# Keeping the convolution's buffers alive across stages, with Q computed row block by row block

## The chip, the cores and the metric

The kernel runs on one core of a Trainium2 chip. The metric is the device time of one execution in microseconds (us); the figure for a kernel is the median of several executions. TensorE (PE) does the matmuls, with its weight loads listed separately (PEld); VectorE (DVE) and ScalarE (ACT) take results out of PSUM and do the elementwise work; SyncE's queue (SP) issues every transfer. The transfers themselves run on 16 DMA engines.

## The reference

One branchformer layer over two sequences, B = 2, T = 4000, D = 512, convolution width K = 31, all in bfloat16. Cut to what matters:

```python
xa = layernorm(x)
q, k, v = split(xa @ w_qkv, 3)
p = softmax(q @ k.T * D**-0.5)
glob = (p @ v) @ w_att_out
h = gelu(layernorm(x) @ w_mlp_in)
u, g = h[..., :D], layernorm(h[..., D:])
gc = depthwise_conv(g, dw_csgu)          # 31 taps along t, each channel by itself
loc = (u * gc) @ w_mlp_out
m = concat(glob, loc)                    # 1024 channels
m = m + depthwise_conv(m, dw_merge)
out = x + m @ w_merge
```

There are two depthwise convolutions: the gate convolution over 512 channels of `g`, and the merge convolution over 1024 channels of `m`.

## The kernel before

For each of the two batches the kernel goes through the same stages, with all of a stage's time steps done before the next one starts:

- P1: load x, layer normalisation in groups of 8 tiles of 128 rows (statistics on VectorE), transpose on TensorE, copy by ScalarE into `xnT` (channels on partitions). Batch 1's P1 is emitted with batch 0's final projection.
- P3: `g` by matmul with `w_in` (`pg`), Gelu, normalisation, store to DRAM (`g_d`); `u` by matmul into `uT`; the gate convolution; then the matmul with `w_mo` and the store of `loc_d`.
- P2: the Q and V projections. W_q times W_k transposed is folded into one matrix `A_sb`, and W_v times the output projection into `Wvo_sb`, so that keys are `xnT` itself.
- Attention: for each of 32 blocks of 128 rows the scores S (8 tiles of up to 512 columns, `pS`), the row maximum on VectorE, Exp on ScalarE in two halves into `Pm`, a DMA transpose of `Pm` into `PT`, and 32 accumulating matmuls of `PT` with `v_sb` (`pO`), whose result `at` is stored to `glob_d`. The emission order puts the scores of the next block, and two tiles of the one after, ahead of PV of the present block.
- P5: the merge convolution over `loc_d` and then `glob_d` into `mconvT`, and the final matmul with `w_mg` (`po`), to which x is added (`xt`, `ot`).

A convolution goes over chunks of 128 channels: 4 chunks for the gate, 8 for the merge. For a chunk, `depthwise` loads `mch` (41 overlapping windows of 128 time steps, 128 channels; 1312 KB in runs of 256 bytes) and eight `tz` tiles. A `tz` tile holds, for 16 channels, the banded matrix that turns the convolution of one channel into one matmul; it is read from a small DRAM array `zz` with overlapping rows, 512 KB a time. Each channel is then one matmul of 41 columns with a weight load of its own (L129), VectorE copies 12 channels at a time into `cm` (L136), and 41 transposes per chunk (L144) bring the result back to channels on partitions.

Every transfer is issued by SP, in program order, with its waits ahead of it. The order within an engine is what a list scheduler made of the emitted program, guided by when tiles come free. Memory is given out by pools that are opened and closed like a stack. The convolution's pools (`mch` 3 buffers, `cm` 2, `tz` 10) are opened anew in each stage and so take addresses that the stage before was using; loads into them can't start before those tenants are done. The same holds for `w_in`, which is placed where P1's buffers were. `qT`, the whole Q of a batch, takes 32 KB per partition all through attention.

Of the kernel before, what the change touches and what calls it, by code (L numbers as in the profile page):

```python
# [11 lines left out]
BF = mybir.dt.bfloat16  # L12
F32 = mybir.dt.float32
PSUM = bass.MemoryType.PSUM

P = 128
# [3 lines left out]
SEG = 128  # L20
LEAD = 112
EPS = 1e-5
CG = 16
TZB = 10
LNG = 8


# [5 lines left out]
def kernel(  # L33
# [40 lines left out]
    A_sb = const.tile([P, KC, D], BF, name="A_sb")  # L74
    Wvo_sb = const.tile([P, KC, D], BF, name="Wvo_sb")

    zz = tc.dram_tile([LEAD + CT * SEG + P], BF, name="zz")
    g_d = [tc.dram_tile([TP, D], BF, name=f"g_d{b}") for b in range(B)]
    glob_d = [tc.dram_tile([TP, D], BF, name=f"glob_d{b}") for b in range(B)]
# [23 lines left out]
    def ln_group(small, src, i0, ni, tagp):  # L103
# [7 lines left out]
        nc.vector.reciprocal(rstd[:, :ni], rstd[:, :ni])  # L111
        return mv, rstd

    def depthwise(sc, ch_base, cc, m_pool, cm_pool, tz_pool, ps_pool):
        src_tl = m_pool.tile([P, NB, P], BF, name="mch")
        nc.sync.dma_start(src_tl[:], halo_chunk_src(sc, cc))
        cm = cm_pool.tile([P, P, NBP], BF, name="cm")
        tzs = []
        for g0 in range(0, P, CG):
            tz = tz_pool.tile([P, CG * SEG], BF, name="tz")  # L120
            nc.sync.dma_start(tz[:], hankel_src(ch_base + cc * P + g0, CG))
            tzs.append(tz)
        for c0 in range(0, P, PB):
            cn = min(PB, P - c0)
            pc = ps_pool.tile([P, PB, NB], F32, name="pc")
            for c in range(c0, c0 + cn):
                tz = tzs[c // CG]
                o = (c % CG) * SEG
                nc.tensor.matmul(  # L129
                    pc[:, c - c0, :],  # L130
                    tz[:, o:o + P],
                    src_tl[:, :, c],
                    start=True,
                    stop=True,
                )
            nc.vector.tensor_copy(cm[:, c0:c0 + cn, :NB], pc[:, :cn, :])  # L136
        return cm
# [13 lines left out]
                emit(SO * n, v, pT[:, nn - 1, P - 1 - PADT:P - 1 - PADT - v:-1], 0)  # L151

    def emit_p1(b, xnT, xp, io, small, ps1):
        x_all = xp.tile([P, NT, D], BF, name="x_all")
        if rem:
            nc.vector.memset(x_all[:, nfull, :], 0.0)
            nc.sync.dma_start(x_all[:rem, nfull, :], x[b, nfull * P:T, :])
        for i0 in range(0, NT, LNG):
            ni = min(LNG, NT - i0)
            nf = min(i0 + ni, nfull) - i0  # L160
            if nf > 0:
                nc.sync.dma_start(
                    x_all[:, i0:i0 + nf, :],
                    x[b, i0 * P:(i0 + nf) * P, :].rearrange("(n p) d -> p n d", p=P),
                )
        for i0 in range(0, NT, LNG):
            ni = min(LNG, NT - i0)
            mv, rstd = ln_group(small, x_all, i0, ni, "x")
            for i in range(i0, i0 + ni):
                r = min(P, T - i * P)  # L170
                xn = io.tile([P, D], BF, name="xn")
                nc.vector.tensor_scalar(
                    xn[:r], x_all[:r, i, :], mv[:r, i - i0, 0:1],
                    rstd[:r, i - i0:i - i0 + 1], ALU.subtract, ALU.mult,
                )
                pt = ps1.tile([P, KC, P], BF, name="pt1")
                for k in range(KC):
                    nc.tensor.transpose(
                        pt[:, k, :r], xn[:r, k * P:(k + 1) * P], ident[:r, :r]
                    )  # L180
                nc.scalar.copy(xnT[:, :, i * P:i * P + r], pt[:, :, :r])  # L181
# [72 lines left out]
    def emit_p3(b, xnT):  # L254
        with tc.tile_pool(name=f"ug{b}", bufs=1) as ug_pool, tc.tile_pool(
# [7 lines left out]
            with tc.tile_pool(name="p3ga", bufs=1) as gap:  # L263
# [24 lines left out]
                for e in range(KC):  # L288
                    for t0 in range(0, T, 512):
# [13 lines left out]
            with tc.tile_pool(name="p3m", bufs=3) as mp, tc.tile_pool(  # L303
                name="p3cm", bufs=2
            ) as cmp_, tc.tile_pool(name="p3tz", bufs=TZB) as tzp, tc.tile_pool(
                name="p3pc", bufs=2, space=PSUM
            ) as psc, tc.tile_pool(name="p3pt", bufs=2, space=PSUM) as pst:
                for cc in range(KC):
                    cm = depthwise(g_d[b], 0, cc, mp, cmp_, tzp, psc)

                    def emit(t0, ln, src, nblk, cc=cc):
                        dst = uT[:, cc, t0:t0 + ln]
                        if nblk:
                            dst = dst.rearrange("p (n s) -> p n s", s=SO)
                        nc.vector.tensor_tensor(dst, src, dst, ALU.mult)

                    conv_to_dlayout(cm, pst, emit)
# [20 lines left out]
                            nc.vector.tensor_copy(l_all[:r, i, :], pl[:r, :])  # L338
                    store_rows(loc_d[b], l_all, i0, ni)

    def emit_p2(b, xnT, qT, v_sb):
        with tc.tile_pool(name="p2ps", bufs=4, space=PSUM) as ps2:
            cnt = 0
            for e in range(KC):
                for t0 in range(0, T, 512):
                    w = min(512, T - t0)
                    pq = ps2.tile([P, 512], F32, name="pq")
                    for k in range(KC):
                        nc.tensor.matmul(  # L349
                            pq[:, :w],  # L350
                            A_sb[:, k, e * P:(e + 1) * P],
                            xnT[:, k, t0:t0 + w],
                            start=(k == 0),
                            stop=(k == KC - 1),
                        )
                    if cnt % 2 == 0:
                        nc.scalar.copy(qT[:, e, t0:t0 + w], pq[:, :w])
                    else:
                        nc.vector.tensor_copy(qT[:, e, t0:t0 + w], pq[:, :w])
                    cnt += 1  # L360
            for i in range(NA):
                r = min(RC, T - i * RC)
                pv = ps2.tile([P, 512], F32, name="pq")
                for k in range(KC):
# [7 lines left out]
                if cnt % 2 == 0:  # L372
# [3 lines left out]
                cnt += 1  # L376

    def emit_attention(b, qT, kT, v_sb):
# [4 lines left out]
        with tc.tile_pool(name="p4s", bufs=2) as sp, tc.tile_pool(  # L383
# [5 lines left out]
        ) as psS, tc.tile_pool(name="p4psT", bufs=(1 if DMAT else 3), space=PSUM) as psT, tc.tile_pool(  # L389
            name="p4psO", bufs=2, space=PSUM  # L390
        ) as psO:
            state = {}
            LEADT = 2 if NS > 4 else 0

            def emit_S(i, j0, j1):
                r = min(RC, T - i * RC)
                if i not in state:
                    state[i] = dict(
                        S=sp.tile([P, T], F32, name="S_sb"),
                        mt=small.tile([P, NS], F32, name="mt"),  # L400
                    )
                S_sb, mt = state[i]["S"], state[i]["mt"]
# [68 lines left out]
            def emit_PV(i):  # L471
# [16 lines left out]
                )  # L488
                del state[i]

            emit_S(0, 0, NS)
            emit_softmax(0)
            if NA > 1:
                emit_S(1, 0, LEADT)
            for i in range(NA):
                if i + 1 < NA:
                    emit_S(i + 1, LEADT, NS)
                    emit_softmax(i + 1)
# [2 lines left out]
                emit_PV(i)  # L501

    def emit_merge_conv(b, mconvT):
        with tc.tile_pool(name="p5m", bufs=3) as mp, tc.tile_pool(
            name="p5cm", bufs=2
        ) as cmp_, tc.tile_pool(name="p5tz", bufs=TZB) as tzp, tc.tile_pool(
            name="p5pc", bufs=3, space=PSUM
        ) as psc, tc.tile_pool(name="p5pt", bufs=3, space=PSUM) as pst:
            for h in (1, 0):
                for cc in range(KC):  # L510
                    cm = depthwise((glob_d, loc_d)[h][b], D + h * D, cc, mp, cmp_, tzp, psc)
# [36 lines left out]
    for b in range(B):  # L548
        emit_p3(b, xnT)
        at_ctx = ExitStack()  # L550
        at_pool = at_ctx.enter_context(tc.tile_pool(name=f"att{b}", bufs=1, side="right"))
        qT = at_pool.tile([P, KC, T], BF, name="qT")
        v_sb = at_pool.tile([P, NA, D], BF, name="v_sb")
        emit_p2(b, xnT, qT, v_sb)
        emit_attention(b, qT, xnT, v_sb)
        at_ctx.close()
        xn_ctx.close()

# [48 lines left out]
```

## Time and profile before

| | before |
|---|---|
| time, median of 5 | 1795.91 us (1792.29 to 1796.77) |
| profiled execution | span 1789.3 us, mean granted TensorE clock 0.905 |
| PE busy | 1657.7 us (93%) |
| DVE, ACT busy | 841.5 us (47%), 574.7 us (32%) |
| transfers | 257.39 MB, mean 144 GB/s; q1 busy 55.5% of 16 engines' span |
| scores L407, PV L477 | 440.7 and 456.9 us busy |
| conv matmuls L129, transposes L144 | 245.2 and 107.1 us busy |

A row of the page's groups gives line, engine, operation, output and inputs, shape and count, then busy time and mean duration, then the time that the engine stood idle just before and what ended it. A busy PE is not PE at its peak: matmuls are pipelined, and their durations overlap, so the spacing of their starts is the price of one. The page's part 2 cuts the span into 40 slices of 44.7 us; a digit is a busy share in tenths. A line of the sums over stretches has start and end, length, the busy time of PE, PEld, DVE, ACT and POOL with the number of instructions in brackets, then the granted clock, the share of the DMA engines and GB/s. A line of the chain of waits has start, length and what the end of the program was waiting for at that time.

### The profile page before, as it was taken

The numbers are of one execution on the slowest core, as the hardware profiler recorded it, in microseconds if no ns is written. First come the engines' busy times: TensorE is split into PE (matmuls) and PEld (weight loads), VectorE is DVE, ScalarE is ACT, GpSimd is POOL, SyncE is SP. The second block draws the span as 40 slices with busy tenths as digits, with TensorE's granted clock in tenths as the row PEclk, the third lists the DMA queues.
The fourth block names the chain that finished last, engine by engine and source line by source line (L and its number), as shares of the span: only waits on it lengthen the run. The fifth ranks groups of instructions, "written<-read, shape, count | busy, mean of one in ns | idle before, by whom it ended". The sixth has DMA issues, their size and how long they took to land.

```text
span 1789.3 us, 25506 instructions
## 1 busy us (share of the span) xinstructions
PE 1657.7 (93%) x10166; PEld 918.6 (51%) x10292; DVE 841.5 (47%) x2093; ACT 574.7 (32%) x782; POOL 13.8 (1%) x72
## 2 busy tenths in 40 slices
PE   5899999999999997978978999999999999978799
PEld 3368444444444443877443774444444444457764
DVE  7636344444444442444747453544444444424333
ACT  6740333333333332212048213333333333321210
POOL 0000000000000000000000000000000000000000
PEclk9986999999999999655979889999999999985569
DMA  5695205444444447998753941244445444489964
GB/s 157 223 228 175 92 0 103 80 86 94 86 80 80 94 91 167 320 315 262 216 205 99 262 143 62 36 94 80 80 89 94 84 80 83 96 262 297 300 220 140
DMA packets 473063, 257.39 MB, mean 144 GB/s; under 512 B 394898, under 2 KB 446801, under 8 KB 472944
## 3 DMA queue, kind: packets, MB, share of 16 engines
q1 hardware_dynamic: 472944, 255.76, 55.5%
q8 instruction: 80, 1.31, 0.3%
q14 instruction: 39, 0.32, 0.1%
HBM read 156.73 MB, written 33.46 MB: 106 GB/s over the span
## 4 chain that ended last, share of the span: by engine, by line
PE 43%; DMA 5%; ACT 2%; DVE 1%; issue 1%; SPq 0%; ACTq 0%; DVEq 0%
PE pS L407 12%; PE pO L477 12%; PE po L528 6%; DMA tz<-zz 4%; PE pc L129 4%; PE pTc L144 3%; PE pq L365 2%; PE pg L328 2%; PE pq L349 2%; PE pg L293 1%; PE pg L273 1%; DVE cm L136 1%; ACT xnT L181 1%; DMA w_in<-in_w_mlp_in_dram 0%; DMA w_mg<-in_w_merge_dram 0%
## 5 line engine op out<-in xcount | busy, mean ns | idle before, releaser
L414 DVE TENSOR_SCALAR_CACHE_REDUCE S_sb<-pS,mt 128x512 f32<-128x512 f32 (+1 forms) x448 | 329.7, 736 | 291.6 <-PE pS L407 243.6
L477 PE MATMUL pO<-v_sb,PT 128*128 128x512 bf16 (+2 forms) x2008 | 456.9, 379 | 6.5 <-DMA PT<-Pm 4.4
L407 PE MATMUL pS<-xnT,qT 128*128 128x512 bf16 (+2 forms) x2008 | 440.7, 374 | 3.7 <-DVE v_sb L375 1.5
L437 ACT ACTIVATE Pm<-S_sb,nb 128x2048 bf16<-128x2048 f32 (+3 forms) x128 | 250.1, 1954 | 365.1 <-DVE nb L428 365.1
L477 PEld LDWEIGHTS <-PT 128*128 128x128 bf16 (+2 forms) x2048 | 199.4, 98 | 266.4 <-issue 28.7
L407 PEld LDWEIGHTS <-qT 128*128 128x128 bf16 (+1 forms) x2048 | 195.1, 98 | 233.5 <-issue 14.3
L136 DVE CAST cm<-pc 128x492 bf16<-128x492 f32 (+1 forms) x264 | 171.5, 657 | 254.0 <-PE pc L129 254.0
L129 PE MATMUL pc<-mch,tz 128*128 128x41 bf16 x3072 | 245.2, 250 | 47.3 <-DMA tz<-zz 46.1
L129 PEld LDWEIGHTS <-tz 128*128 128x128 bf16 x3072 | 223.5, 120 | 68.0 <-DMA tz<-zz 44.5
L517 ACT COPY mconvT<-pTc 128x784 bf16<-128x784 bf16 x96 | 65.8, 718 | 224.5 <-PE pTc L144 222.5
L144 PE MATMUL pTc<-ident,cm 128*128 128x128 bf16 x984 | 107.1, 298 | 14.3 <-DVE cm L136 13.1
L485 ACT ACTIVATE at<-pO,rl 128x512 bf16<-128x512 f32 x64 | 44.0, 687 | 228.5 <-PE pO L477 220.4
L528 PE MATMUL po<-w_mg,mconvT 128*128 128x512 bf16 (+1 forms) x500 | 110.8, 379 | 4.0 <-DVE ot L538 2.1
L144 PEld LDWEIGHTS <-cm 128*128 128x128 bf16 x984 | 100.2, 161 | 18.7 <-DVE cm L136 17.3
L451 DVE TENSOR_REDUCE rl<-lp 128x1 f32<-128x2 f32 x64 | 9.9, 154 | 170.4 <-ACT Pm L437 170.4
L528 PEld LDWEIGHTS <-mconvT 128*128 128x128 bf16 (+1 forms) x512 | 49.9, 98 | 63.7 <-issue 5.0
L273 PE MATMUL pg<-w_in,xnT 128*128 128x512 bf16 (+1 forms) x251 | 59.9, 395 | 19.0 <-ACT g_all L280 9.7
L538 DVE TENSOR_TENSOR ot<-po,xt 128x512 bf16<-128x512 f32 x64 | 43.7, 687 | 54.3 <-PE po L528 48.9
L336 ACT CAST l_all<-pg 128x512 bf16<-128x512 f32 x32 | 18.6, 586 | 151.7 <-PE pTc L144 119.0
L328 PE MATMUL pg<-w_mo,uT 128*128 128x512 bf16 (+1 forms) x246 | 57.4, 382 | 1.3 <-ACT l_all L336 1.0
L293 PE MATMUL pg<-xnT,w_in 128*128 128x512 bf16 (+1 forms) x250 | 54.3, 374 | 3.5 <-ACT uT L300 3.2
L365 PE MATMUL pq<-Wvo_sb,xnT 128*128 128x512 bf16 (+1 forms) x252 | 55.6, 379 | 0.2
(62 smaller groups left out, 836.2 us busy)
## 6 DMA issues: line engine op xcount, KB each, us to landing
tz<-zz SPq DMA_DIRECT2D x192, 512.0 KB, 8.2
mch<-g_d SPq DMA_DIRECT2D x8, 1312.0 KB, 13.9
mch<-loc_d SPq DMA_DIRECT2D x8, 1312.0 KB, 9.1
mch<-glob_d SPq DMA_DIRECT2D x8, 1312.0 KB, 15.8
glob_d<-at SPq DMA_DIRECT2D x62, 128.0 KB, 1.7
xt<-in_x_dram SPq DMA_DIRECT2D x62, 128.0 KB, 2.3
out_dram<-ot SPq DMA_DIRECT2D x62, 128.0 KB, 1.7
x_all<-in_x_dram SPq DMA_DIRECT2D x6, 1024.0 KB, 5.8
```

The costliest lines, as they stand in the source:

```text
L129: nc.tensor.matmul(pc[:, c - c0, :], tz[:, o:o + P], src_tl[:, :, c], start=True, stop=True,)
L136: nc.vector.tensor_copy(cm[:, c0:c0 + cn, :NB], pc[:, :cn, :])
L144: nc.tensor.transpose(pT[:, n - n0, :], cm[:, :, n], ident[:])
L273: nc.tensor.matmul(pg[:r, :], xnT[:, k, i * P:i * P + r], w_in[:, k, D:2 * D], start=(k == 0), stop=(k == KC - 1),)
L293: nc.tensor.matmul(pu[:, :w], w_in[:, k, e * P:(e + 1) * P], xnT[:, k, t0:t0 + w], start=(k == 0), stop=(k == KC - 1),)
L328: nc.tensor.matmul(pl[:r, :], uT[:, k, i * P:i * P + r], w_mo[:, k, :], start=(k == 0), stop=(k == KC - 1),)
L365: nc.tensor.matmul(pv[:r, :D], xnT[:, k, i * RC:i * RC + r], Wvo_sb[:, k, :], start=(k == 0), stop=(k == KC - 1),)
L407: nc.tensor.matmul(pS[:r, :w], qT[:, k, i * RC:i * RC + r], kT[:, k, s0:s0 + w], start=(k == 0), stop=(k == KC - 1),)
L414: nc.vector.tensor_scalar(S_sb[:r, s0:s0 + w], pS[:r, :w], 1.0, mt[:r, j - 1:j] if j > 0 else None, ALU.mult, ALU.max, accum_out=mt[:r, j: ...
L437: nc.scalar.activation(Pm[:r, c0:c0 + w], S_sb[:r, c0:c0 + w], ACT.Exp, bias=nb_[:r], scale=scale, accum_out=lp[:r, ci:ci + 1],)
L477: nc.tensor.matmul(pO[:r, :], PT[:sr, c, :r], v_sb[:sr, c, :], start=(c == 0), stop=(c == NA - 1),)
L528: nc.tensor.matmul(po[:r, :], mconvT[:, cc, i * P:i * P + r], w_mg[:, cc, :], start=(cc == 0), stop=(cc == 2 * KC - 1),)
```

## The change

Three edits that share one memory budget.

1. `mch` (now 2 buffers) and ten `tz` buffers come from pools that are opened once for the whole program. Each convolution stage opens a small pool of three more `tz` buffers; `depthwise` takes ten tiles from the lasting pool, then three from the small one, and so on. A convolution's first loads can be issued while earlier stages still run.
2. To pay for that, `qT` goes. P2 computes V alone; attention computes Q for one block of 128 rows (`emit_Q`: 16 matmuls of 128 columns into one PSUM bank, one ScalarE copy into `qb`) two blocks ahead of use. PSUM for this bank is taken from the score tiles, which have 4 buffers instead of 5.
3. P1 no longer holds all of x (`x_all`, 32 KB per partition) but three buffers of 8 tiles (`xg`, 24 KB).

```diff
+    cv_m = ctx.enter_context(tc.tile_pool(name="cvm", bufs=2))
+    cv_tz = ctx.enter_context(tc.tile_pool(name="cvtz", bufs=TZB))
...
         for g0 in range(0, P, CG):
-            tz = tz_pool.tile([P, CG * SEG], BF, name="tz")
+            if isinstance(tz_pool, tuple):
+                pool_, n_p, n_x = tz_pool[0], tz_pool[1], tz_pool[2]
+                k_ = tz_cnt[0] % (n_p + n_x)
+                tz_cnt[0] += 1
+                tzp_ = pool_[0] if k_ < n_p else pool_[1]
...
     def emit_p1(b, xnT, xp, io, small, ps1):
-        x_all = xp.tile([P, NT, D], BF, name="x_all")
...
+            xg = xp.tile([P, LNG, D], BF, name="xg")
...
-        xp = stack.enter_context(tc.tile_pool(name="p1x", bufs=1))
+        xp = stack.enter_context(tc.tile_pool(name="p1x", bufs=3))
...
-            with tc.tile_pool(name="p3m", bufs=3) as mp, tc.tile_pool(
-                name="p3cm", bufs=2
-            ) as cmp_, tc.tile_pool(name="p3tz", bufs=TZB) as tzp, tc.tile_pool(
+            with tc.tile_pool(name="p3cm", bufs=2) as cv_cm, tc.tile_pool(name="p3tzx", bufs=TZX) as tzx, tc.tile_pool(
...
-            for e in range(KC):
-                for t0 in range(0, T, 512):
-                    w = min(512, T - t0)
-                    pq = ps2.tile([P, 512], F32, name="pq")
...
-                            A_sb[:, k, e * P:(e + 1) * P],
-                            xnT[:, k, t0:t0 + w],
...
-            name="p4psS", bufs=(5 if DMAT else 3), space=PSUM
+            name="p4psQ", bufs=1, space=PSUM
+        ) as psQ, tc.tile_pool(
+            name="p4psS", bufs=(4 if DMAT else 3), space=PSUM
...
+            def emit_Q(i):
+                r = min(RC, T - i * RC)
+                pq = psQ.tile([P, KC, P], F32, name="pq4")
+                for e in range(KC):
+                    for k in range(KC):
+                        nc.tensor.matmul(
+                            pq[:, e, :r],
+                            A_sb[:, k, e * P:(e + 1) * P],
+                            kT[:, k, i * RC:i * RC + r],
+                            start=(k == 0),
+                            stop=(k == KC - 1),
+                        )
+                qb = wk.tile([P, KC, P], BF, name="qb")
+                nc.scalar.copy(qb[:, :, :r], pq[:, :, :r])
+                qbs[i] = qb
...
-                            qT[:, k, i * RC:i * RC + r],
+                            qb[:, k, :r],
...
             for i in range(NA):
+                if i + 2 < NA:
+                    emit_Q(i + 2)
                 if i + 1 < NA:
```

The merge convolution's pools change as the gate's do (p5m, p5cm and p5tz before; p5cm and p5tzx, three buffers, after).

More of the change, by code (lines that the diff above doesn't have):

```diff
@@ L24 @@
 TZB = 10
+TZX = 3
 LNG = 8
@@ L112, in ln_group @@
         return mv, rstd
+    tz_cnt = [0]
     def depthwise(sc, ch_base, cc, m_pool, cm_pool, tz_pool, ps_pool):
@@ L119, in depthwise @@
         for g0 in range(0, P, CG):
-            tz = tz_pool.tile([P, CG * SEG], BF, name="tz")
+            if isinstance(tz_pool, tuple):
[3 more added lines that the diff above has]
+                tzp_ = pool_[0] if k_ < n_p else pool_[1]
+            else:
+                tzp_ = tz_pool
+            tz = tzp_.tile([P, CG * SEG], BF, name="tz")
             nc.sync.dma_start(tz[:], hankel_src(ch_base + cc * P + g0, CG))
@@ L153, in emit_p1 @@
     def emit_p1(b, xnT, xp, io, small, ps1):
-        x_all = xp.tile([P, NT, D], BF, name="x_all")
-        if rem:
-            nc.vector.memset(x_all[:, nfull, :], 0.0)
-            nc.sync.dma_start(x_all[:rem, nfull, :], x[b, nfull * P:T, :])
         for i0 in range(0, NT, LNG):
@@ L160, in emit_p1 @@
             nf = min(i0 + ni, nfull) - i0
+            xg = xp.tile([P, LNG, D], BF, name="xg")
             if nf > 0:
                 nc.sync.dma_start(
-                    x_all[:, i0:i0 + nf, :],
+                    xg[:, :nf, :],
                     x[b, i0 * P:(i0 + nf) * P, :].rearrange("(n p) d -> p n d", p=P),
                 )
-        for i0 in range(0, NT, LNG):
-            ni = min(LNG, NT - i0)
-            mv, rstd = ln_group(small, x_all, i0, ni, "x")
+            if i0 + ni > nfull and rem:
+                nc.vector.memset(xg[:, nfull - i0, :], 0.0)
+                nc.sync.dma_start(xg[:rem, nfull - i0, :], x[b, nfull * P:T, :])
+            mv, rstd = ln_group(small, xg, 0, ni, "x")
             for i in range(i0, i0 + ni):
@@ L172, in emit_p1 @@
                 nc.vector.tensor_scalar(
-                    xn[:r], x_all[:r, i, :], mv[:r, i - i0, 0:1],
+                    xn[:r], xg[:r, i - i0, :], mv[:r, i - i0, 0:1],
                     rstd[:r, i - i0:i - i0 + 1], ALU.subtract, ALU.mult,
@@ L302, in emit_p3 @@
                         )
-            with tc.tile_pool(name="p3m", bufs=3) as mp, tc.tile_pool(
-                name="p3cm", bufs=2
-            ) as cmp_, tc.tile_pool(name="p3tz", bufs=TZB) as tzp, tc.tile_pool(
+            with tc.tile_pool(name="p3cm", bufs=2) as cv_cm, tc.tile_pool(name="p3tzx", bufs=TZX) as tzx, tc.tile_pool(
                 name="p3pc", bufs=2, space=PSUM
             ) as psc, tc.tile_pool(name="p3pt", bufs=2, space=PSUM) as pst:
+                tz_cnt[0] = 0
                 for cc in range(KC):
-                    cm = depthwise(g_d[b], 0, cc, mp, cmp_, tzp, psc)
+                    cm = depthwise(g_d[b], 0, cc, cv_m, cv_cm, ((cv_tz, tzx), TZB, TZX), psc)
                     def emit(t0, ln, src, nblk, cc=cc):
@@ L339, in emit_p3, with emit_p2 @@
                     store_rows(loc_d[b], l_all, i0, ni)
-    def emit_p2(b, xnT, qT, v_sb):
+    def emit_p2(b, xnT, v_sb):
         with tc.tile_pool(name="p2ps", bufs=4, space=PSUM) as ps2:
-            cnt = 0
-            for e in range(KC):
-                for t0 in range(0, T, 512):
-                    w = min(512, T - t0)
-                    pq = ps2.tile([P, 512], F32, name="pq")
-                    for k in range(KC):
-                        nc.tensor.matmul(
-                            pq[:, :w],
-                            A_sb[:, k, e * P:(e + 1) * P],
-                            xnT[:, k, t0:t0 + w],
[L353 to L360, printed above, removed]
             for i in range(NA):
@@ L371, in emit_p2 @@
                     )
-                if cnt % 2 == 0:
+                if i % 2 == 0:
                     nc.scalar.copy(v_sb[:r, i, :], pv[:r, :D])
@@ L375, in emit_p2, with emit_attention @@
                     nc.vector.tensor_copy(v_sb[:r, i, :], pv[:r, :D])
-                cnt += 1
-    def emit_attention(b, qT, kT, v_sb):
+    def emit_attention(b, kT, v_sb):
         s_tiles = [(s0, min(512, T - s0)) for s0 in range(0, T, 512)]
@@ L387, in emit_attention @@
         ) as small, tc.tile_pool(name="p4wk", bufs=3) as wk, tc.tile_pool(
-            name="p4psS", bufs=(5 if DMAT else 3), space=PSUM
-        ) as psS, tc.tile_pool(name="p4psT", bufs=(1 if DMAT else 3), space=PSUM) as psT, tc.tile_pool(
+            name="p4psQ", bufs=1, space=PSUM
+        ) as psQ, tc.tile_pool(
+            name="p4psS", bufs=(4 if DMAT else 3), space=PSUM
+        ) as psS, tc.tile_pool(name="p4psT", bufs=(1 if DMAT else 2), space=PSUM) as psT, tc.tile_pool(
             name="p4psO", bufs=2, space=PSUM
@@ L393, in emit_attention @@
             LEADT = 2 if NS > 4 else 0
+            qbs = {}
+            def emit_Q(i):
[13 more added lines that the diff above has]
+                qbs[i] = qb
             def emit_S(i, j0, j1):
@@ L397, in emit_S @@
                 if i not in state:
+                    if i not in qbs:
+                        emit_Q(i)
                     state[i] = dict(
@@ L400, in emit_S @@
                         mt=small.tile([P, NS], F32, name="mt"),
+                        qb=qbs.pop(i),
                     )
-                S_sb, mt = state[i]["S"], state[i]["mt"]
+                S_sb, mt, qb = state[i]["S"], state[i]["mt"], state[i]["qb"]
                 for j in range(j0, j1):
@@ L489, in emit_PV @@
                 del state[i]
+            emit_Q(0)
+            if NA > 1:
+                emit_Q(1)
             emit_S(0, 0, NS)
@@ L503, in emit_merge_conv @@
     def emit_merge_conv(b, mconvT):
-        with tc.tile_pool(name="p5m", bufs=3) as mp, tc.tile_pool(
-            name="p5cm", bufs=2
-        ) as cmp_, tc.tile_pool(name="p5tz", bufs=TZB) as tzp, tc.tile_pool(
+        with tc.tile_pool(name="p5cm", bufs=2) as cv_cm, tc.tile_pool(name="p5tzx", bufs=TZX) as tzx, tc.tile_pool(
             name="p5pc", bufs=3, space=PSUM
         ) as psc, tc.tile_pool(name="p5pt", bufs=3, space=PSUM) as pst:
+            tz_cnt[0] = 0
             for h in (1, 0):
                 for cc in range(KC):
-                    cm = depthwise((glob_d, loc_d)[h][b], D + h * D, cc, mp, cmp_, tzp, psc)
+                    cm = depthwise((glob_d, loc_d)[h][b], D + h * D, cc, cv_m, cv_cm, ((cv_tz, tzx), TZB, TZX), psc)
                     def emit(t0, ln, src, nblk, ch=h * KC + cc):
@@ L551 @@
         at_pool = at_ctx.enter_context(tc.tile_pool(name=f"att{b}", bufs=1, side="right"))
-        qT = at_pool.tile([P, KC, T], BF, name="qT")
         v_sb = at_pool.tile([P, NA, D], BF, name="v_sb")
-        emit_p2(b, xnT, qT, v_sb)
-        emit_attention(b, qT, xnT, v_sb)
+        emit_p2(b, xnT, v_sb)
+        emit_attention(b, xnT, v_sb)
         at_ctx.close()
```

## The prediction

> **What bounds the kernel now.** I read the page first: part 2 for the stages, part 4 for what the end waits on.
>
> ```profile
> PE   5899999999999997978978999999999999978799
> PEclk9986999999999999655979889999999999985569
> DMA  5695205444444447998753941244445444489964
> PE 43%; DMA 5%; ACT 2%; DVE 1%; issue 1%; SPq 0%; ACTq 0%; DVEq 0%
> ```
>
> TensorE is the bound nearly everywhere. The exception shows as columns where PE drops to 7 or 8, its clock to 5 or 6 and DMA rises to 9: slices 16 to 18 and 36 to 38, the merge convolutions. The sums over stretches (us, then busy time of PE, PEld, DVE, ACT, POOL, granted clock, DMA share, GB/s) price the stages: the P2 projections, the merge convolution of each batch, and the gate convolution of batch 1.
>
> ```profile
> 202.00:250.00 48.00, 47.23 (x218) 21.87 (x224) 18.72 (x28) 16.26 (x28) 0.30 (x2) 1.00 0.06 21
> 705.00:852.00 147.00, 116.08 (x1354) 106.11 (x1354) 57.65 (x90) 33.50 (x49) 0.00 (x0) 0.59 0.96 295
> 1000.00:1060.00 60.00, 57.06 (x675) 54.19 (x677) 40.54 (x69) 1.07 (x2) 0.00 (x0) 0.72 0.67 220
> 1587.00:1731.00 144.00, 117.20 (x1352) 106.60 (x1354) 57.11 (x88) 32.79 (x48) 0.00 (x0) 0.57 0.97 301
> ```
>
> In the merge convolution the DMA share is 0.96 and 0.97: transfers are the limit, and in P2 they stand idle (0.06). The chain of waits shows how the stage opens and goes on in batch 1, and PE's timeline the waits in batch 0:
>
> ```profile
> 1579.68 7.19 PE pO L477 x32
> 1586.88 5.39 DMA w_mg<-in_w_merge_dram
> ...
> 1592.66 10.73 DMA tz<-zz
> 1603.43 0.76 PE pc L129 x8
> ...
> 1620.70 9.45 DMA tz<-zz
> ```
>
> ```profile
> 697.83 7.18 PE L477 MATMUL pO<-v_sb,PT 128*32 128x512 bf16 x32 [2.83 <-DMA PT<-Pm]
> 712.51 1.32 PE L129 MATMUL pc<-mch,tz 128*128 128x41 bf16 x16 [7.50 <-DMA tz<-zz]
> ```
>
> After the last attention matmul PE stands 7.5 us, then each chunk waits for `tz` again. The load sizes (page, part 6) and the matmul rates (PE's timeline: start, duration, count):
>
> ```profile
> tz<-zz SPq DMA_DIRECT2D x192, 512.0 KB, 8.2
> mch<-loc_d SPq DMA_DIRECT2D x8, 1312.0 KB, 9.1
> ```
>
> ```profile
> 36.02 0.39 PE L178 MATMUL pt<-ident,xn 128*128 128x128 bf16 x4
> 36.25 0.66 PE L248 MATMUL pa<-wao_sb,wT 128*128 128x512 bf16 x2
> ...
> 202.51 27.16 PE L349 MATMUL pq<-xnT,A_sb 128*128 128x512 bf16 x125 [0.77 <-DVE l_all L338]
> ```
>
> Four 128-column matmuls, each with its own weight load, take 36.25 - 36.02 = 0.23 us: 57 ns each (55 is the median spacing of starts at L178 at full clock, 107 at half). 512 columns take 216. The last line is the Q projection, 27.2 us a batch.
>
> Between the batches PE also waits for `w_in`:
>
> ```profile
> 910.70 7.98 ACT xnT L181 x15
> ...
> 929.39 5.47 DMA w_in<-in_w_mlp_in_dram
> ```
>
> [...]
>
> **The change part by part.**
>
> *Q by rows.* P2 loses 128 matmuls of 512 columns: -27.2 us a batch. Attention gains 16 matmuls of 128 columns for each of 31 full row blocks and a short one: 31 x 16 x 0.0555 = 27.5, plus 0.6 for the short block and 0.4 to start: +28.5. Net +1.3, twice +2.6 us. The eviction `qb` (128x512 on ScalarE, 0.59 as in the L336 row) stands behind `at` and ahead of the next Exp on the strict queue; both come just after PV, and the first use of `qb` is 24 matmuls (5.2 us) later. Exp waits for S longer than that, so nothing on the path. ScalarE is 1/3 busy. `pS` goes from 5 buffers to 4: VectorE takes 0.75 + 0.08 + gaps = 0.88 a tile against PE's 0.86, and between bursts PE spends 6.9 us in PV, so four suffice: 0.
>
> *Pools that outlive the stages.* The order of the changed program puts ten `tz` and two `mch` loads of the merge convolution ahead of attention; three more `tz` follow when the score buffers come free. Their tenants before lay where attention's buffers were. Time from the last PV matmul, T. One chunk is 8 `tz` + 1 `mch` = 5408 KB, and it takes 18.0 us in batch 1 (transposes at 1636.02 to 1725.96, five chunks) and 18.5 in batch 0: take 18.3, all transfer. PE starts at T. Chunk 0 is done at T + 10 (128 x 73 ns + 0.6); `w_mg` and the few `tz` whose buffers come free meanwhile load beside it. The third `mch` must now wait for chunk 0's last matmul, because `mch` has 2 buffers instead of 3; everything behind it on SP waits too. From there six chunks are to be moved: 6 x 18.3 = 110, to T + 120. The last 16 matmuls, the eviction, 41 transposes and a ScalarE copy take 1.2 + 0.6 + 4.5 + 1.0: T + 127.3. PE alone would need 8 x 15.1 = 121 (the gate convolution runs four chunks in 60.5), so transfers still end it, barely. Before: 704.9 to 851.9 = 147.0, and 1586.9 to 1731.1 = 144.2. Gain 19.7 + 16.9 = 36.6 us.
>
> In the gate convolution (PE-bound) the third `mch` is issued at +10, its chunk is complete by about +28.5, and PE wants it at +30; chunk 3 by +47 for a use from +45 to +55. Just hidden: 0.
>
> *x in groups of 8 tiles.* `w_in` no longer waits for P1's end: its waits are now only older transfers and, in batch 1, the last `po` matmul. At the start PE waited for it until 51.83, 3.3 us after the last matmul of the weight products; P1's own work ends near 47 to 48, so -4. Between the batches the 5.5 us wait goes. In exchange all 32 tiles' transposes stand behind the final projection (before, 30 of them: 18.9 us, 0.63 each on ScalarE): 20.2; and the fourth group's load waits for group 0's normalisation, while its first statistics stand ahead of group 2's normalisation on VectorE: about +3. Before 24.4 us from the last `po` to the first `pg`, after 23.3: -1. The x loads start one transpose block earlier, which saves perhaps 1 of PE's 2.4 idle us in the final; ten prefetched `tz` share that stretch (DMA share 0.5 there). Together -2.
>
> Sum: -36.6 + 2.6 - 4 - 2 = -40: 1795.9 - 40 = 1756.
>
> **The rivals.**
> A. *Q is dearer.* In the convolution a pair of weight load and 41-column matmul is spaced 73 ns[...]. Against it: the conv's moving operand is strided, L178's isn't, and L178 runs at 55.
> B. *The stage gains more.* The transfers at 720 us, with `tz` alone, ran at 384 to 399 GB/s; if less waiting lets a chunk through in 16.6 us, the stage ends at T + 117: 10 more each, 1736. For it: the packets' own times. Against: 18.3 held over ten chunks at a share of 1.0.
> C. *Slower: `mch` starves PE.* `mch` takes 14.9 us (median) to land and now leaves only after a whole chunk. If the transfers idle 3.3 us in each of the six fed chunks, both gains are gone (+40), and if in the gate convolutions the two late chunks are 4 us late each, +16: 1812. Against it: when transfers are the limit a chunk's worth is always queued.
> D. *Same*: half of C, 1796.
>
> **How the numbers follow.** My forecast 0.62, A 0.15, B 0.16, C 0.05, D 0.02. The range runs from B's 1736 to just over A's lower price, 1778; outside lie A's dear end, C, D and a deeper B, under 2 in 10. Faster 0.93 (forecast, A, B), same 0.02, slower 0.05.
>
> **What would show it.** The merge convolution from last PV to first `po` near 127 us, without the 7.5 us hole; PE's waits for `tz` inside it few until the last chunks; `pq4` matmuls spaced 55 to 57 ns; the first `pg` before 49 us; no wait for `w_in` at the second P1. I'd be wrong if the DMA share falls well under 0.9 in the stage, if PE waits for `mch` in the gate convolution, or if an attention row block takes over 15.1 us instead of 13.9 + 0.9.

## The result, and the profile after

| | before | after |
|---|---|---|
| median of the executions compared | 1794.35 us (15) | 1751.88 us (8; 1750.14 to 1755.34) |
| ratio to before, 95% interval | | 0.9763 (0.9754 to 0.9773) |
| profiled execution | 1789.3 us, clock 0.905 | 1750.9 us, clock 0.918 |

The change takes 42.5 us off the medians and 38.4 us off the profiled executions; the forecast was 40. The tables and lines below are of the profiled executions, so the stages add up to the 38.4. The changed kernel's page, parts 2, 4, 5 and 6 (busy tenths; shares of the chain; groups with busy time, mean ns and idle time before them; transfers with KB and median us to landing):

```profile
PE   5899999999999999988978999999999999999899
...
PEclk9987999999999999656979889999999999996679
DMA  7488724444444444999733985444444444449964
...
PE 80%; DMA 7%; SPq 6%; ACT 4%; DVE 2%; issue 1%; DVEq 0%; ACTq 0%
...
L491 PE MATMUL pO<-v_sb,PT 128*128 128x512 bf16 (+2 forms) x2014 | 456.4, 379 | 2.2 <-issue 0.6
...
L142 PE MATMUL pc<-mch,tz 128*128 128x41 bf16 x3072 | 240.1, 250 | 21.0 <-DMA tz<-zz 19.9
...
L395 PE MATMUL pq<-xnT,A_sb 128*128 128x128 bf16 (+1 forms) x1024 | 67.2, 218 | 3.0 <-DVE v_sb L367 1.5
...
tz<-zz SPq DMA_DIRECT2D x192, 512.0 KB, 7.9
...
mch<-glob_d SPq DMA_DIRECT2D x8, 1312.0 KB, 16.6
```

PE's dip at the merge convolutions is shallower, but the slices with DMA at 9 are still there. The convolution's idle time before its matmuls (L142) is 21.0 us; the same group stood at 47.3 before, 46.1 of it for `tz`. The PV group's idle time went from 6.5 to 2.2. So most of the gain lies in that one wait, and some of the wait is left. The two rows before:

```profile
L477 PE MATMUL pO<-v_sb,PT 128*128 128x512 bf16 (+2 forms) x2008 | 456.9, 379 | 6.5 <-DMA PT<-Pm 4.4
...
L129 PE MATMUL pc<-mch,tz 128*128 128x41 bf16 x3072 | 245.2, 250 | 47.3 <-DMA tz<-zz 46.1
```

The sums over stretches: V projection, merge of batch 0, gate convolution of batch 1, merge of batch 1 (columns as in the prediction's table).

```profile
195.00:225.00 30.00, 28.77 (x130) 12.66 (x132) 11.32 (x17) 9.96 (x17) 0.30 (x2) 1.00 0.63 122
698.00:829.00 131.00, 114.42 (x1355) 107.32 (x1355) 57.28 (x89) 33.71 (x50) 0.00 (x0) 0.62 0.99 297
976.00:1037.00 61.00, 58.56 (x688) 55.86 (x689) 39.96 (x67) 0.82 (x3) 0.00 (x0) 0.72 0.88 278
1565.00:1692.00 127.00, 113.39 (x1345) 106.48 (x1346) 57.11 (x88) 32.15 (x47) 0.00 (x0) 0.62 0.95 284
```

The rate in the merge stage is what it was (297 and 284 GB/s, before 295 and 301) and the DMA share still near 1. The stage is shorter because there is less left to move in it: 38.8 and 36.1 MB in place of 43.3 in both batches, by the packets of those stretches (the 38.8 include 1.7 of the next batch's x). The rest went ahead: the ten `tz` in the gate convolution and just behind it (share 0.88 in the line above, 0.67 before), and the two `mch` in the V projection, where the share, 0.06 before in P2, is now 0.63. On SP's timeline of batch 0 (eight of the sixteen `tz` in its first row are the gate's own):

```profile
134.52 27.48 SPq L134 DMA_DIRECT2D tz<-zz  x16
176.41 1.79 SPq L134 DMA_DIRECT2D tz<-zz  x2
200.15 5.66 SPq L122 DMA_DIRECT2D mch<-loc_d  x2
```

PE's timeline of the changed kernel (start, duration, count, and in brackets the wait before it), from the start, attention and the merge of batch 0, and the second P1:

```profile
46.39 12.21 PE L284 MATMUL pg<-w_in,xnT 128*128 128x512 bf16 x47 [0.41 <-ACT xnT L192]
...
310.37 1.07 PE L395 MATMUL pq<-xnT,A_sb 128*128 128x128 bf16 x16
311.28 6.91 PE L421 MATMUL pS<-xnT,qb 128*128 128x512 bf16 x31
...
689.67 8.67 PE L491 MATMUL pO<-v_sb,PT 128*128 128x512 bf16 x38
698.27 11.25 PE L142 MATMUL pc<-mch,tz 128*128 128x41 bf16 x152
...
725.89 9.52 PE L142 MATMUL pc<-mch,tz 128*128 128x41 bf16 x128
...
740.13 9.49 PE L142 MATMUL pc<-mch,tz 128*128 128x41 bf16 x128
...
810.11 1.33 PE L142 MATMUL pc<-mch,tz 128*128 128x41 bf16 x16 [1.85 <-DMA tz<-zz]
...
821.51 1.32 PE L142 MATMUL pc<-mch,tz 128*128 128x41 bf16 x16 [1.40 <-DMA tz<-zz]
...
898.00 1.04 PE L189 MATMUL pt<-ident,xn 128*128 128x128 bf16 x8 [2.07 <-DVE xn L183]
...
906.18 1.03 PE L189 MATMUL pt<-ident,xn 128*128 128x128 bf16 x8 [3.31 <-DVE xn L183]
```

The convolution (698.27) begins as PV ends (689.67 + 8.67 = 698.34): the 7.5 us hole is gone. The first four chunks start at 0, 9.2, 27.6 and 41.8 us after the last PV and run with no wait for `tz`; the later ones wait again, by up to 1.85 us at a time. The `pq` group before scores (310.37) takes 0.91 us for 16 matmuls up to the next start.

Put together by stage, from the traces (us; the first column ends at the first `pg`, the merge runs from the last PV to the first `po`, "P1" is from the last `po` to the next `pg`):

| | to first pg | g, u | gate conv | P2 and attention | merge | final | P1 | g, u | gate conv | P2 and attention | merge | final |
|---|---|---|---|---|---|---|---|---|---|---|---|---|
| before | 51.8 | 63.5 | 86.4 | 503.3 | 146.9 | 58.6 | 24.4 | 64.0 | 85.9 | 502.0 | 143.8 | 55.5 |
| after | 46.4 | 63.6 | 86.0 | 502.3 | 130.6 | 58.8 | 23.7 | 64.8 | 86.7 | 502.3 | 127.2 | 55.4 |

"Gate conv" includes the `w_mo` matmul. The merge gives 16.3 + 16.6 = 32.9 of the 38.4 us, the start 5.4.

### The profile page after: what moved, and what is told of

It is laid out like the page before. It is cut to its first block, busy times and chain, and to the rows that moved or that the text cites. A ratio compares the mean times of both kernels' runs of the same rounds, so it can differ in the third digit from the quotient of the medians.

```text
span 1750.9 us, 26950 instructions
## 1 busy us (share of the span) xinstructions
PE 1652.7 (94%) x10925; PEld 950.2 (54%) x11060; DVE 819.9 (47%) x2061; ACT 590.8 (34%) x814; POOL 13.8 (1%) x72
## 4 chain that ended last, share of the span: by engine, by line
PE 80%; DMA 7%; SPq 6%; ACT 4%; DVE 2%; issue 1%; DVEq 0%; ACTq 0%
PE pO L491 26%; PE pS L421 25%; PE pc L142 7%; SPq L134 6%; DMA tz<-zz 5%; PE po L546 4%; PE pq L395 4%; PE pq L357 3%; PE pg L338 3%; PE pTc L157 3%; PE pg L304 3%; PE pg L284 3%; DMA xt<-in_x_dram 1%; ACT xnT L192 1%; DMA dwsb<-in_dw_merge_dram 1%
## 5 line engine op out<-in xcount | busy, mean ns | idle before, releaser
L421 PE MATMUL pS<-xnT,qb 128*128 128x512 bf16 (+2 forms) x1988 | 439.3, 374 | 3.2
L421 PEld LDWEIGHTS <-qb 128*128 128x128 bf16 (+1 forms) x2048 | 197.3, 98 | 217.3 <-issue 1.1
L142 PE MATMUL pc<-mch,tz 128*128 128x41 bf16 x3072 | 240.1, 250 | 21.0 <-DMA tz<-zz 19.9
L142 PEld LDWEIGHTS <-tz 128*128 128x128 bf16 x3072 | 224.7, 120 | 34.7 <-DMA tz<-zz 28.7
L395 PE MATMUL pq<-xnT,A_sb 128*128 128x128 bf16 (+1 forms) x1024 | 67.2, 218 | 3.0 <-DVE v_sb L367 1.5
L346 ACT CAST l_all<-pg 128x512 bf16<-128x512 f32 x32 | 18.6, 586 | 152.1 <-PE pTc L157 119.4
L395 PEld LDWEIGHTS <-A_sb 128*128 128x128 bf16 x1024 | 56.7, 98 | 17.8 <-issue 14.8
## 6 DMA issues: line engine op xcount, KB each, us to landing
mch<-glob_d SPq DMA_DIRECT2D x8, 1312.0 KB, 16.6
xg<-in_x_dram SPq DMA_DIRECT2D x6, 1024.0 KB, 10.7
```

The lines of the kernel that those rows point to most:

```text
L142: nc.tensor.matmul(pc[:, c - c0, :], tz[:, o:o + P], src_tl[:, :, c], start=True, stop=True,)
L395: nc.tensor.matmul(pq[:, e, :r], A_sb[:, k, e * P:(e + 1) * P], kT[:, k, i * RC:i * RC + r], start=(k == 0), stop=(k == KC - 1),)
L421: nc.tensor.matmul(pS[:r, :w], qb[:, k, :r], kT[:, k, s0:s0 + w], start=(k == 0), stop=(k == KC - 1),)
```

## The experiments

Eight kernels were run. The theory: the merge stage is a queue of transfers, and the change shortens it by taking bytes out of it, at a small price for Q. The rivals: the gain is only the hole at the stage's start; the gain comes from P1 or Q; or PE has become the bound.

**Q by rows alone**, on the kernel before (`q_only`).

```diff
-                    pq = ps2.tile([P, 512], F32, name="pq")
+            def emit_Q(i):
...
+                pq = psQ.tile([P, KC, P], F32, name="pq4")
```

> The kernel before with the Q edit alone (Q by row blocks, score tiles 5 to 4 buffers). Theory: the 128-column matmuls cost the same per column, so P2 gives up 27 us a batch and attention takes 27 to 28: the time of before within 3 us (about 1794), P2 and attention together 502 to 505 us a batch, merge convolution still 144 to 147. Rival: the row blocks are themselves a gain or a loss of over 5 us, which the other edits hid.

Measured 1796.12 us, ratio 1.0008 (1.0000 to 1.0017). P2 and attention took 504.7 and 504.2, so +1.4 and +2.2 against before, where +1.3 each was worked out. The matmuls of L395 start 56 ns apart (median of 962 pairs in the changed kernel). The rival, a gain or a loss of over 5 us, falls: the Q edit by itself buys nothing and costs nearly nothing. PE's timeline of this kernel, Q and the last PV:

```profile
301.97 1.07 PE L385 MATMUL pq<-xnT,A_sb 128*128 128x128 bf16 x16
...
699.90 7.18 PE L481 MATMUL pO<-v_sb,PT 128*32 128x512 bf16 x32 [2.33 <-DMA PT<-Pm]
714.70 1.32 PE L129 MATMUL pc<-mch,tz 128*128 128x41 bf16 x16 [7.61 <-DMA tz<-zz]
```

The wait of 2.33 us for `PT` before the last PV is also in the kernel before (2.83) and not in the changed one; in batch 1 it is 1.77 here, 1.58 before and nothing in the changed kernel.

**P1 in groups alone**, on the kernel before (`xg_only`).

```diff
-        x_all = xp.tile([P, NT, D], BF, name="x_all")
...
+            xg = xp.tile([P, LNG, D], BF, name="xg")
...
-        xp = stack.enter_context(tc.tile_pool(name="p1x", bufs=1))
+        xp = stack.enter_context(tc.tile_pool(name="p1x", bufs=3))
```

> The kernel before with the P1 edit alone (x in three buffers of 8 tiles). Theory: w_in is no longer placed in P1's memory, the first pg starts near 46.4 us instead of 51.8 and the second P1 is about 1 us shorter: 1788 us, 6 less than before. Rival: the early w_in came from the lasting pools, which moved the layout: 1794, first pg at 51.8.

Measured 1785.8 us, ratio 0.9956 (0.9940 to 0.9971). The first `pg`, on PE's timeline:

```profile
48.29 2.54 PE L271 MATMUL pg<-w_in,xnT 128*128 128x512 bf16 x11 [0.41 <-ACT xnT L179]
```

It starts 3.5 us earlier than before and no longer waits for `w_in`, so the rival falls; 46.4 was expected. In this kernel g, u and the final of batch 0 are 1.1 and 1.4 us shorter too. The edit brings 8.6 us where 6 were expected. In the changed kernel these two stages are not shorter (63.6 and 58.8 us); of the final more is told below, for g and u the cause stays open.

**All the edits, but pools opened in each stage** (`stage_pools`): same counts of buffers as the changed kernel, `mch` 2 and `tz` 10 + 3, at addresses that the stage before uses.

```diff
-    cv_m = ctx.enter_context(tc.tile_pool(name="cvm", bufs=2))
-    cv_tz = ctx.enter_context(tc.tile_pool(name="cvtz", bufs=TZB))
...
+        with tc.tile_pool(name="p5m", bufs=2) as cv_m, tc.tile_pool(name="p5cm", bufs=2) as cv_cm, tc.tile_pool(name="p5tz", bufs=TZB) as cv_tz, tc.tile_pool(name="p5tzx", bufs=TZX) as tzx, tc.tile_pool(
```

> The changed kernel with mch (2 buffers) and tz (10 and 3) opened anew in each convolution stage. Transfer theory: no load of the merge convolution but mch comes early, so the merge stage is back at 144 to 147 us and the kernel at about 1787. Rival: the deeper set of 13 tz buffers brings the gain, wherever it lives: merge stage near 130, kernel 1752 to 1760. A third: with only 2 mch buffers the stage is longer than before, over 150, and the kernel over 1795.

Measured 1788.54 us, ratio 0.9963 (0.9948 to 0.9978). PE's timeline at the end of attention, then the two merge stretches:

```profile
693.16 7.18 PE L489 MATMUL pO<-v_sb,PT 128*32 128x512 bf16 x32 [2.44 <-DMA PT<-Pm]
707.94 10.61 PE L140 MATMUL pc<-mch,tz 128*128 128x41 bf16 x128 [7.60 <-DMA tz<-zz]
```

```profile
700.00:847.00 147.00, 116.42 (x1355) 105.69 (x1356) 57.40 (x89) 33.73 (x50) 0.00 (x0) 0.62 0.96 295
1583.00:1727.00 144.00, 117.69 (x1356) 106.91 (x1357) 57.13 (x88) 32.99 (x48) 0.00 (x0) 0.59 0.97 301
```

The hole is back, and the merge stages take 146.3 and 143.1 us, within 0.7 of the kernel before. The rival of the deeper set of 13 `tz` falls, and so does the third. The lifetime of the pools alone is worth 1788.54 - 1751.88 = 36.7 us; the other two edits, which pay its memory, bring the 5.8 us that are left (P1 in groups by itself 8.6).

**Fewer lasting `tz` buffers** (`tz6`): the hole still closes, but four `tz` fewer are ahead.

```diff
-TZB = 10
+TZB = 6
```

> The changed kernel with 6 lasting tz buffers instead of 10 (three more in the stage, as before). Transfer theory: time saved is transfers moved ahead of the stage, so the four tz that are no longer loaded early cost 4 x 1.3 = 5.3 us in each merge convolution: 136 and 132, kernel about 1762; a shorter tail of prefetches in the first final projection gives back up to 1. Rival (the gain is the hole of 7.5 us at the stage's start, which six tz and two mch fill as well): merge stages as with ten, kernel 1752.

Measured 1759.74 us, ratio 0.9814 (0.9799 to 0.9828); the merge took 135.1 and 131.9 us, 4.5 and 4.7 more than the changed kernel's. Its two merge stretches (from the last PV, rounded to a whole us):

```profile
697.00:832.00 135.00, 115.54 (x1354) 107.07 (x1354) 59.59 (x94) 33.49 (x48) 0.00 (x0) 0.57 1.01 306
1567.00:1699.00 132.00, 114.61 (x1350) 105.86 (x1350) 57.13 (x88) 32.39 (x47) 0.00 (x0) 0.58 0.96 290
```

Every `tz` that isn't there ahead of time comes back as 1.1 to 1.2 us of stage. A gain from the hole alone would have left the stage as it was: that rival falls.

**Half of the bytes of each `tz` load** (`half_tz`).

```diff
-            nc.sync.dma_start(tz[:], hankel_src(ch_base + cc * P + g0, CG))
+            nc.sync.dma_start(tz[:, :CG // 2 * SEG], hankel_src(ch_base + cc * P + g0, CG // 2))
...
-                o = (c % CG) * SEG
+                o = (c % (CG // 2)) * SEG
```

> The changed kernel, but each tz load brings 8 channels' matrices instead of 16 and both halves of the matmuls use them: it leaves out half of the convolution weights, with the same number of instructions. Transfer theory: the last four chunks of the merge stage stop waiting, all eight take the 14.3 us of chunks 2 and 3, and the stage takes about 116 us instead of 131 and 127: 26 less in all, 1726 us; the gate convolution stays at 60 us. Rival (PE is already the limit): merge stage 127 to 131, kernel 1752.

Measured 1715.31 us, ratio 0.9564 (0.9549 to 0.9579), merge 113.7 and 113.5. Its merge stretches:

```profile
695.00:809.00 114.00, 108.99 (x1354) 107.28 (x1354) 57.13 (x88) 33.31 (x49) 0.00 (x0) 0.66 0.89 221
1540.00:1654.00 114.00, 109.60 (x1354) 108.00 (x1355) 57.13 (x88) 32.63 (x47) 0.00 (x0) 0.66 0.82 199
```

This kernel leaves out half of the convolution's weights; only its time is of use. At 199 to 221 GB/s PE waits for no `tz` at all and is busy 109 of 114 us: this is PE's own length for the stage, with the same number of matmuls. It is 14 to 17 us less than the changed kernel's stage, so transfers still end that one, and the rival falls. The expectation was 116.

**One more `mch`, two lasting `tz` fewer** (`mch3_tz8`). By the packet times in the changed kernel's merge, an `mch` load is 128 x 41 = 5248 packets of 256 bytes at 23.4 ns on 16 engines, 7.7 us, and a `tz` load 128 packets of 4096 bytes at 171 ns, 1.37 us. A chunk is then 7.7 + 8 x 1.37 = 18.6 us, as its period of 18.5 shows, and `mch`, a quarter of its bytes, is 41% of it. A third `mch` ahead is worth more than two `tz`.

```diff
-TZB = 10
-TZX = 3
+TZB = 8
+TZX = 5
...
-    cv_m = ctx.enter_context(tc.tile_pool(name="cvm", bufs=2))
+    cv_m = ctx.enter_context(tc.tile_pool(name="cvm", bufs=3))
```

> The changed kernel with 3 lasting mch buffers and 8 lasting tz, 5 more tz in the stage (13 tz as before). Transfer theory: one more mch ahead of the stage is worth 7.5 us of transfers, two tz fewer cost 2.7, so each merge stage is about 4.8 us shorter: 126 and 122, kernel about 1742. Rival (a blocked mch on the issuing queue is what costs): over 8 us shorter in each merge stage and some in the gate convolution as well, under 1735. Third: nothing, 1752.

Measured 1737.74 us, ratio 0.9694 (0.9675 to 0.9714); merge 123.9 and 121.5, which is 6.7 and 5.7 less than the changed kernel. The packet price, 7.7 - 2 x 1.37 = 5.0, was to be had, and 0.7 to 1.7 us more came. The rival asked for over 8 us in each and for a gain in the gate convolution (86.8 and 87.6 us, none); it falls, though the little that came on top is not explained. The two merge stretches:

```profile
698.00:822.00 124.00, 112.94 (x1353) 108.01 (x1353) 57.13 (x88) 33.76 (x49) 0.00 (x0) 0.61 1.00 310
1555.00:1676.00 121.00, 112.62 (x1347) 108.17 (x1347) 57.13 (x88) 32.90 (x47) 0.00 (x0) 0.59 0.95 294
```

**One `mch` load for two chunks** (`mch_pair`), in runs of 512 bytes instead of 256.

```diff
-        return bass.AP(sc.tensor, sc.offset + cc * P, [[D, P], [SO * D, NB], [1, P]])
+        return bass.AP(sc.tensor, sc.offset + cc * P, [[D, P], [SO * D, NB], [1, 2 * P]])
...
-        src_tl = m_pool.tile([P, NB, P], BF, name="mch")
-        nc.sync.dma_start(src_tl[:], halo_chunk_src(sc, cc))
+        if cc % 2 == 0:
+            pair[0] = m_pool.tile([P, NB, 2 * P], BF, name="mch")
+            nc.sync.dma_start(pair[0][:], halo_chunk_src(sc, cc))
+        src_tl = pair[0]
+        cb = (cc % 2) * P
```

`TZB` is 5 and `TZX` 8, to pay for the larger `mch`.

> The changed kernel with one mch load for two chunks (256 channels, runs of 512 bytes instead of 256; two such buffers) and 5 lasting tz, 8 more in the stage. Transfer theory: four chunks' mch are there before the merge stage, and in it some 99 us of transfers are left, less than PE's own time, so the stage ends on PE as in the run with halved tz: about 116 us, kernel about 1728; the gate convolution unchanged. Rival: wider rows slow the strided read of the matmul or the loads queue badly in front of the gate convolution: merge stage not under 125.

Measured 1716.76 us, ratio 0.9572 (0.9557 to 0.9586); merge 112.8 and 111.7. Its merge stretches:

```profile
699.00:812.00 113.00, 108.44 (x1354) 106.97 (x1354) 57.31 (x89) 33.56 (x50) 0.00 (x0) 0.68 0.94 339
1544.00:1656.00 112.00, 108.20 (x1353) 106.77 (x1354) 57.13 (x88) 32.31 (x47) 0.00 (x0) 0.69 0.89 322
```

The same matmuls and the full weights now take what `half_tz` took: PE busy 108 of 112 us, no wait for `tz`. Transfers are off the path, and this version beats both kernels, the changed one by 35 us. Two things came together in it. A packet of 512 bytes took 32.7 ns here, so the `mch` of two chunks takes 5248 x 32.7 / 16 = 10.7 us instead of 15.4. From that and the times above, an estimate: two more chunks' `mch` held ahead take 15.4 us of transfers out of the stage, the cheaper loads of the last four chunks 9.2, and the five `tz` fewer put 6.8 back. No run parts them.

**Transposes later** (`pair_late`): on top of `mch_pair`, the transposes of a chunk are emitted after the first 24 channels of the next, to hide PE's last regular gap, 0.6 us for `cm` in most chunks.

```diff
-                    conv_to_dlayout(cm, pst, emit)
+                    def prev(cm=cm, emit=emit):
+                        conv_to_dlayout(cm, pst, emit)
+            prev()
```

> As the run with paired mch loads, with each chunk's transposes emitted after the first 24 channels of the next chunk, so that PE doesn't stand 0.6 us for the last copy of cm. If the stages are bound by PE by then: 0.6 us for each of about 20 chunks, 10 to 12 us less than the paired run, about 1717. If transfers still end the merge stage, only the gate convolution's share: 3 us.

Measured 1717.56 us, ratio 0.9579 (0.9563 to 0.9595): no gain. That this is the expected 1717 is chance, since the paired run itself came out at 1717 instead of 1728. PE's timeline shows why nothing was gained:

```profile
737.06 0.32 PE L163 MATMUL pTc<-ident,cm 128*128 128x128 bf16 x1 [0.60 <-DVE cm L153]
737.18 1.35 PE L146 MATMUL pc<-mch,tz 128*128 128x41 bf16 x16
```

The scheduler put one transpose of the finished chunk ahead of the next chunk's matmuls, and that one still waits for `cm`; in other chunks all 41 still stand ahead. Emission order is not issue order here, so the idea itself stays untried.

## Why the prediction was right

**The merge convolution.** Predicted -36.6, measured -32.9. The mechanism is shown from three sides: the gain vanishes when the pools are opened in the stage, returns in part with six lasting `tz`, and goes further when more `mch` is held ahead or its loads get cheaper. The stage's end was put at T + 127.3; batch 1 ended at 127.2, batch 0 at 130.6. In batch 1 the steps hold as well: the third `mch` left at T + 9.5 (put at 10), and the last `tz` packet ended at T + 120.7 (put at 120). The term that was mis-sized is the end of batch 0, and it is not the price of a chunk: the last chunk's matmuls start at T + 111.8 in batch 0 and at 111.9 in batch 1. What differs comes after that. In batch 0 the last 16 matmuls wait once more for `tz` (1.40 us) and the final matmul starts 6.4 us after the last of them started; in batch 1 they don't wait, and it is 5.2. SP issues ten `tz` with the last chunk of batch 0, two of them for the next gate convolution, which the prediction missed. SP's timeline in batch 0, and PE's at the last chunk of batch 1 (that of batch 0 is shown above, from 810.11 on):

```profile
793.80 18.78 SPq L134 DMA_DIRECT2D tz<-zz  x10
```

```profile
1677.14 10.33 PE L142 MATMUL pc<-mch,tz 128*128 128x41 bf16 x128 [2.24 <-DMA tz<-zz]
```

But the kernel before and `stage_pools`, which issue no such two, show the same split: their last chunks start within 0.4 us of each other, and batch 0 ends 3.1 and 3.2 us later, against 3.4 here. So the two `tz` cost little, and the cause of the longer end stays open. The prediction's 18.5 and 18.0 us a chunk hold this difference, as means up to the last chunk's transposes, and it took the middle. It also took the stage of batch 1 before as 144.2; to the first `po` it is 143.8.

"PE alone would need 121, so transfers still end it, barely" had the right order with the wrong margin: with transfers out of the way PE took 112 to 114. The 15.1 us a chunk came from a gate convolution in whose 60.5 us nine matmuls with `w_mo` stand too; up to the next start they take 3.0 us. Without them a chunk is 14.4, and eight are 115. PE's timeline of before has the first of them:

```profile
1015.29 0.61 PE L328 MATMUL pg<-w_mo,uT 128*128 128x512 bf16 x2
```

The clock explains neither this margin nor the gain. It was at half for 34.1 of 60.6 us in that gate convolution and for 71.7 of 112.8 in the merge of `mch_pair`, which is the faster of the two by the chunk. A pair of weight load and 41-column matmul takes 73 ns at either clock; a transpose takes 107 ns at half and 63 at full, but most stand at half in either kernel (before 279 of 318 spacings in the merge of batch 0, changed 295 of 318).

**Q by rows.** Predicted +2.6; by itself +3.6 in these stages (`q_only`), with starts 56 ns apart where 55.5 was used. Rival A is settled: its lower price was the 73 ns of the convolution's pairs, by which 1000 Q matmuls would cost 1000 x (73 - 55.5) = 17.5 us more and the kernel 1773. Its dear end, above that, was an assumption that no trace shows. But P2 and attention of the changed kernel together moved by -1.0 and +0.3, not +1.3 each. Against `q_only` that is -2.4 and -1.9, the length of the wait for `PT` that is gone from the end of attention (2.33 and 1.77 us there; 1.58 to 2.83 in all four kernels whose `mch` loads start there, none in the six with `mch` loaded long before). The prediction named that line of the trace only for the hole after it: the transposed `PT` of the last blocks had been in the same queue as the first `mch`.

**The start.** Predicted -4, measured -5.4 by the first `pg` at 46.4. P1 by itself gives 48.3, and so does `stage_pools` (48.4); with lasting pools it is 46.4 to 46.9 in four kernels, but 48.2 and 48.4 in `mch_pair` and `pair_late`, which have such pools too. So 1.9 us of the start are not P1's, and their cause stays open.

**Final and second P1.** Predicted -2, measured -0.5. P1 went -0.7 as against -1: the `w_in` wait is gone and two stalls on `xn` of 2.07 and 3.31 us stand in its place (before, one of 1.63): the fourth group's load and statistics, which the prediction put at about 3. The final of batch 0 didn't gain (+0.2), although with P1 alone it does (-1.4). VectorE's timeline of the final in the changed kernel:

```profile
845.36 0.69 DVE L556 TENSOR_TENSOR ot<-po,xt 128x512 bf16<-128x512 f32 x1 [0.20 <-DMA xt<-in_x_dram]
...
849.96 0.69 DVE L556 TENSOR_TENSOR ot<-po,xt 128x512 bf16<-128x512 f32 x1 [1.22 <-DMA xt<-in_x_dram]
```

The addition of x waits for `xt`, which shares the queue with the prefetched `tz`, and PE shows three gaps of 1.53, 0.86 and 0.47 us there. Kernels without an early `tz` in that stage have gaps as well: two of 1.45 and 0.67 before, one of 1.36 with P1 alone, two of 0.39 and 1.30 in `stage_pools`. With five, six or eight lasting `tz` none is longer than 0.25. Against `stage_pools`, where the pools alone differ, the final is 1.3 us longer: that is what the early loads give back in the next stage. That sharing the queue is the reason is read from the trace; no run tests it by itself, and `tz6`, whose gaps are gone, still has a final of 57.4 us, 3.9 of them at the half clock.

**Gate convolution.** Predicted 0, measured -0.4 and +0.8. Its stretch is 61 us long as before 60, PE busy 58.6: two `mch` suffice there, so rival C, starved chunks, did not come. In the merge stage C's 3.3 us of idle transfers per chunk did not come either (DMA share 0.99 and 0.95).

**Rival B**, a chunk in 16.6 us, is what neither batch did; 18.6 is what the packets cost. T + 117 and below was reached only in `half_tz` and in the two kernels with paired `mch` loads, with other packets.

Sum by the profiled executions: -32.9 (merge) - 0.7 (P2 and attention) - 5.4 (start) - 0.5 (final, P1) - 0.1 (last final) and +1.3 in the gate convolutions and g, u together: -38.3. The merge was 3.7 us short of its forecast, and P2 with attention 3.3 better than its own, through a wait that the prediction didn't count: that the sum came so near is in part luck.

## What to carry to other kernels

When a stage is bound by transfers and an earlier stage leaves the queue idle, what counts is how much of its transfers can be moved before it starts. That is set by how many buffers lie at addresses that are free then: the same counts opened inside the stage left it at 146.3 and 143.1 us, and four `tz` buffers fewer cost 4.5. Price the loads of such a stage in packet time rather than in bytes before choosing which to hold ahead; here the load with a quarter of the bytes was two fifths of the time, and holding more of it ahead, in longer runs, took off another 35 us. Once it is prefetched, look at the stage that the early loads now share a queue with; here the final of batch 0 was 1.3 us longer than with pools opened in the stage.

## What the runs showed of the hardware

- Packets in the merge stage took 23.4 ns (256 bytes) and 171 ns (4096; 173 in batch 0) of one engine's time in the changed kernel, and 32.7 ns (512) in `mch_pair`, so here one of 512 cost 30% less than two of 256.
- A load that waited on SP held those behind it. In the changed kernel's merge of batch 0 SP issued nothing from 702.27 to 707.79, when the third `mch` left; the next `tz` left at 708.22, though by an estimate from PE's timeline (698.27 plus 64 matmuls of 73 ns) its buffer, that of chunk 0's fourth `tz`, was free from 702.9 on.
- Sixteen pairs of weight load and 128-column matmul kept 56 ns a start inside attention (median of 962 pairs in the changed kernel). Longer streams of them weren't run.
- Matmuls overlap in the records: in the kernel before, those of PV with 512 columns last 379 ns on the mean and start 216 ns apart, those of the convolution with 41 columns last 250 and start 73 apart.
- With PE busy 96% of the stage (`mch_pair`) the granted clock there was still 0.68 and 0.69, and 0.57 to 0.62 where it waited for `tz`. Being busy with 41-column matmuls and transposes did not bring the full clock here.
- A pair of weight load and 41-column matmul started every 73 ns at the half and at the full clock (gate convolution before: 215 and 284 spacings, the same median).
